# An attention kernel on one core: VectorE planned with its measured pace, and 84 instead of 62 score banks evaluated on it

## The chip, the cores and the metric

The kernel runs on one core of one Trainium2 chip. The metric is the time on the device in microseconds (us), of the whole program. A run is called fast or slow by its state; all runs told here, of every kernel, were in the fast state. Several chips were used, and runs of one call share a chip and the runs of the kernel before on it. PE is TensorE, DVE is VectorE, ACT is ScalarE, POOL is GpSimd, SP is SyncE.

## The reference, cut to what matters

```python
# A: full attention, 16 heads of 28, one shared k and v for all heads; S = 2048, D = 448
q = (x @ wq).reshape(B, S, H, Dh).transpose(0, 2, 1, 3)
k, v = x @ wk, x @ wv
scores = einsum("bhqd,bkd->bhqk", q, k) * Dh ** -0.5
o = einsum("bhqk,bkd->bhqd", softmax(scores), v)
a = o.transpose(0, 2, 1, 3).reshape(B, S, H * Dh) @ wo
# B: sliding attention, 16 heads, window of 8 keys with distance 2, own x, wqkv, wo
b = ...
return concatenate([a, b], axis=-1)
```

A has 16 x 2048 x 2048 exponentials. They decide the time; B is done beside them.

## The kernel before

The scores of A lie in PSUM as 1024 banks of 128 x 512. TensorE writes them into a ring of two slots, of three and of two banks, in turn; one round is both slots. ScalarE reads a slot and writes the exponentials in bf16. 64 banks (one chunk of 512 rows, four heads) are a group; there are 16 groups of about 27 us each.

In some rounds the third bank of the larger slot goes to VectorE, which evaluates the exponential by arithmetic on the bits: one eviction per bank, then three operations of 1024 columns for each two banks. `OFF_AT` says in which rounds of which group:

```python
OFF_AT = {q: (0, 2, 5, 7) for q in range(1, 16)}          # four banks in groups 1 to 15
OFF_AT.update({q: (0, 2, 3, 5, 7, 8) for q in (7,)})       # six in group 7; none in group 0: 62
...
def d_exp(self, bank, slot, sib):
    ...
    o = a("dve", t_dve_ps(512), lambda e: e.tensor_scalar(out=xx[...], in0=g.bank(bank),
        scalar1=-128.0 * A2, scalar2=128.0 * (129 + EOFF), op0=ALU.mult, op1=ALU.add),
        R=[("ring", slot)], W=[("d_x", m % 2, h)], pr=-45)
    if h:                                                   # after the second bank of a pair
        a("dve", t_dve_1x(1024), ... scalar_tensor_tensor(out=u, in0=lo, ...), pr=PSTT)
        a("dve", t_dve_1x(1024), ... scalar_tensor_tensor(out=v, in0=u, ...), pr=PSTT)
        a("dve", t_dve_1x(1024), ... scalar_tensor_tensor(out=out, in0=v, ...), pr=PSTT)
```

The order of the instructions on each engine is made when the kernel is built, by a list scheduler in the kernel. It knows each operation's duration only as a booked constant, takes the ready operation with the lowest `pr`, and lets nothing start on VectorE that would run past the next eviction of the ring by more than `EPS`. At run time the orders are fixed, and semaphores do the rest: an operation whose input is late holds up everything behind it on its engine.

```python
class Sched:
    LATS = {"pe": 0.12, "act": 0.18, "dve": 0.08}           # from an end to the waiting engine
    EPS = 0.03
    OWN = 0.06                                              # from an end to the same engine
...
def t_dve_ps(n): return 0.15 + 1.04e-3 * n
def t_dve_1x(n): return Lock(0.16 + 1.04e-3 * n)
def t_dve_2x(n): return Lock(0.16 + 0.52e-3 * n)
```

Three pieces of the start matter below: the load of the larger part of the query weights, which GpSimd issues and which is booked to land 4 us after its issue; the copies `wq4` of these weights; and the evictions of the keys, in four chunks.

```python
a("gp", 1.5, wload(g.wq, g.A_wq, KC, D), ..., W=[("wq", 1)], dsem="i_wq", land=4, pr=-7.5, ninc=2)
...
for t in range(4):
    a("dve", Lock(0.3), ... tensor_copy(out=g.wq4[:, t], in_=g.wq[...]),
      R=[("wq", min(t, 1)), ...], W=[("wq4", t)], pr=-6 if t == 0 else 1.2 + t)
...
for c in range(4):                                          # key chunks
    pr = -9 if c == 0 else c
    a("dve", t_dve_ps(512), ... tensor_copy(out=kc, in_=g.bank(u.bank)), W=[("kT", c)], pr=pr)   # c > 0
```

The queries of a group are made the same way while the group before it runs: four matmuls, an eviction into `qT`, a square, one more matmul, and a second eviction with an addition.

The softmax here doesn't subtract the row's maximum and nothing guards it: scores larger than these inputs give would overflow.

Of the kernel before, what the change touches and what calls it, by code (L numbers as in the profile page):

```python
# [6 lines left out]
ALU = mybir.AluOpType  # L7
# [7 lines left out]
DH = 28  # L15
# [22 lines left out]
A2 = SCALE * 1.4426950408889634  # L38
OFF_AT = {q: (0, 2, 5, 7) for q in range(1, 16)}
OFF_AT.update({q: (0, 2, 3, 5, 7, 8) for q in (7,)})  # L40
OFF_AT[15] = (0, 2, 3, 5)
LATE = 2
PSTT = -1.5
# [51 lines left out]
class Sched:  # L95
    LAT = 0.13
    LATS = {"pe": 0.12, "act": 0.18, "dve": 0.08}
    MODE = 0.09
# [6 lines left out]
    QKT = 0.315  # L105
    EPS = 0.03
    FILL = None
    OWN = 0.06

# [266 lines left out]
def t_dve_ps(n):  # L376
    return 0.15 + 1.04e-3 * n


def t_dve_1x(n):  # L380
    return Lock(0.16 + 1.04e-3 * n)


def t_dve_2x(n):
    return Lock(0.16 + 0.52e-3 * n)

# [13 lines left out]
class Gen:  # L400
# [185 lines left out]
    def loads(self):  # L586
# [23 lines left out]
        for c in range(NCH):  # L610
            for t in range(4):
                a("sp", 1.3, one(lambda e, c=c, t=t: e.dma_start(
                    out=g.xT_B[:, t, 512 * c:512 * c + 512], in_=g.B_x[0, 512 * c:512 * c + 512, XB0[t]:XB0[t] + 128],
                    transpose=True)), W=[("xT_B", c, t)], dsem=f"i_xb{c}.{t}", land=4.5, pr=-16 + c)
        a("sp", 1.2, lambda e: [
# [19 lines left out]
        for t in range(4):  # L635
            a("dve", Lock(0.3), lambda e, t=t: e.tensor_copy(  # L636
                out=g.wq4[:, t, :, :].rearrange("p k (j e) -> p k j e", j=4)[:, :, :, 0:DH],
                in_=g.wq[:, :, KC * t:KC * t + KC].rearrange("p k (j d) -> p k j d", d=DH)),
              R=[("wq", min(t, 1)), "wqz", ("d_x", 0, 0), ("d_x", 0, 1)], W=[("wq4", t)], pr=-6 if t == 0 else 1.2 + t)
# [5 lines left out]
    def a_head(self):  # L645
# [6 lines left out]
        for c in range(NCH):  # L652
# [11 lines left out]
            if c == 0:  # L664
                a("act", t_act(512), lambda e, u=u, ksq=ksq: e.activation(ksq, g.bank(u.bank), ACT.Square),
                  R=[u, "d_u"], W=[("k_sq", c % 2)], use=u, pr=-100)
            else:
                kc = g.kT[:, 512 * c:512 * c + 512]
                a("dve", t_dve_ps(512), lambda e, u=u, kc=kc: e.tensor_copy(out=kc, in_=g.bank(u.bank)),
                  R=[u], W=[("kT", c)], use=u, pr=pr)  # L670
                a("dve", t_dve_2x(512), lambda e, ksq=ksq, kc=kc: e.tensor_tensor(out=ksq, in0=kc, in1=kc, op=ALU.mult),
                  R=[("kT", c), "d_u"], W=[("k_sq", c % 2)], pr=pr)
            a("pe", t_mm(512), lambda e, u=u, ksq=ksq: e.matmul(g.bank(u.bank), g.hq[:, 2, :], ksq, start=False, stop=True, skip_group_check=True),
# [3 lines left out]
                out=kc, in0=g.bank(u.bank), scalar1=g.cols[:, 0:1], scalar2=None, op0=ALU.add),  # L677
              R=["kadd"], W=[("kT", c)], use=u, pr=pr)
            g.kz_ops[c] = [a("dve", Lock(0.29), lambda e, j=j, c=c, kc=kc: e.tensor_scalar(
                out=g.kz[:, j, 512 * c:512 * c + 512], in0=kc, scalar1=g.cols[:, 8 + j:9 + j], scalar2=None, op0=ALU.mult),  # L680
# [5 lines left out]
    def a_tr(self, c):  # L686

        g, a = self, self.s.add
        for kts in ((0,), (1,), (2,), (3,)) if c == 0 else ((0, 1), (2, 3)):
# [7 lines left out]
            for i, kt in enumerate(kts):  # L697
                dst = g.xT_A[:, kt, 512 * c:512 * c + 512]
                src = lambda u=u, i=i: g.psb[:, 1024 * u.bank + 512 * i:1024 * u.bank + 512 * i + 512]
                if c or kt % 2:  # L700
                    a("dve", 0.42, lambda e, src=src, dst=dst: e.tensor_copy(out=dst, in_=src()),
                      W=[("xT", c, kt)], use=u, pr=-2 if c else -9)
                else:
                    a("act", t_act(512), lambda e, src=src, dst=dst: e.activation(dst, src(), ACT.Copy),
                      W=[("xT", c, kt)], use=u, pr=-110)

    def a_v(self, c):
# [12 lines left out]
        for b in range(4):  # L720
# [11 lines left out]
            in1=gc.unsqueeze(2).to_broadcast([128, 4, DH]), op=ALU.mult),  # L732
          R=[("gcol", c), "v_zero"], W=[("v_aug", 0, c)], use=u, pr=pr)
        a("dve", Lock(0.15), lambda e: e.tensor_scalar(
# [194 lines left out]
    def a_quad_end(self, sc, t, hf=None):  # L929
# [12 lines left out]
        pt = g.PV_T[:, t % 2, :].rearrange("p (b e) -> p b e", e=32)  # L942
        a("dve", 0.25, lambda e: e.reciprocal(out=g.rden[:, t % 2, bs], in_=pt[:, bs, DH]), R=kk("PV"), W=kk("rden"), pr=p0)
        a("dve", t_dve_1x(w), lambda e: e.tensor_tensor(
            out=g.oN[:, bs, :], in0=pt[:, bs, :], in1=g.rden[:, t % 2, bs].unsqueeze(2).to_broadcast([128, b, 32]), op=ALU.mult),
          R=kk("PV") + kk("rden"), W=[("oN", x) for x in keys], pr=p0)
        a("dve", 0.12 + 1.04e-3 * w, lambda e: e.transpose(  # L947
            out=g.oTn[:, t, cs], in_=g.oN[:, :, :].rearrange("p b e -> p (b e)")[:, cs]),
# [28 lines left out]
    B0 = 22.0  # L977
    BSTEP = 23.6

# [90 lines left out]
    def b_soft(self, k2):  # L1070
# [8 lines left out]
          R=[("lg2", par, 0), ("lg2", par, 1)], W=[("e_t", par)], pr=-60)  # L1079
        a("dve", t_dve_1x(256), lambda e: e.tensor_reduce(out=g.ssum[:, :, :], in_=ew, axis=AX.X, op=ALU.add),  # L1080
          R=[("e_t", par)], W=["ssum"], pr=pr)
        a("dve", 0.3, lambda e: e.reciprocal(out=mm(g.rs), in_=mm(g.ssum)), R=["ssum"], W=["rs"], pr=pr)
        for b in range(2):
            a("dve", 0.32, lambda e, b=b: e.tensor_tensor(
                out=g.a_n[:, par, b], in0=g.e_t[:, par, b],
# [76 lines left out]
```

## Time and profile before

| kernel before | |
|---|---|
| median of 3 runs | 460.9 us (460.38 to 461.02) |
| span of the profiled run | 458.8 us |
| first exponential starts, last one ends | 12.03 us, 453.04 us |
| stalls between them | 7.1 us |
| rest of the span (tail) | 5.8 us |

The stalls are worked out from the starts in the trace: the time from one ScalarE instruction to the next, less the time when nothing holds it (904 ns for 1024 columns, 1330 for 1536; 306 and 54 for B's and the key sums' small ones). A stall counts here even where the instructions still overlap in the profile, which the column "idle before" does not show. The views that carry the reading stand in the prediction and are not shown twice. One more is needed later, the busy time of each engine in stretches of the span; the columns are the stretch, its length, busy us (and instructions) of PE, PEld, DVE, ACT and POOL, the granted clock, and the transfers.

```profile
0.00:27.00 27.00, 23.24 (x178) 9.88 (x179) 17.17 (x52) 18.85 (x21) 14.15 (x35) 1.00 1.08 202
27.00:54.00 27.00, 25.12 (x195) 8.61 (x193) 16.31 (x29) 27.00 (x28) 0.40 (x2) 1.00 0.25 43
54.00:441.00 387.00, 367.81 (x3318) 143.06 (x3317) 335.67 (x526) 386.92 (x371) 0.00 (x0) 1.00 0.16 52
```

From 27 us on ScalarE has no gap at all at this scale, and in the first 54 us VectorE is busy for a good half of the time.

### The profile page before, as it was taken

The page shows a single profiled execution, that of the slowest core. Times are in us where ns is not written, and L with a number is a line of the kernel's source. Part 1 is how long each engine was busy: PE and PEld are TensorE (multiplying, and loading weights), DVE is VectorE, ACT ScalarE, POOL GpSimd, SP SyncE. Part 2 cuts the span into 40 slices and gives each one's busy share as a digit, 9 for nine tenths or more (in the row PEclk, how much of TensorE's full clock was granted, in tenths as well). Part 3 has the DMA queues.
Part 4 walks back from the last instruction along what each step waited for, and adds up shares of the span by engine and source line. Part 5 has one row for each costly group of instructions (what it writes and reads, how often), then busy time and mean ns, then how long its engine had stood idle before and what let it go on. Part 6 is the DMA issues. An engine that isn't in the chain of part 4 may idle for free.

```text
span 458.8 us, 8985 instructions
## 1 busy us (share of the span) xinstructions
PE 427.7 (93%) x3818; PEld 165.8 (36%) x3818; DVE 373.9 (81%) x617; ACT 445.3 (97%) x429; POOL 14.6 (3%) x37
## 2 busy tenths in 40 slices
PE   7999898899999999999999999999998998989984
PEld 3333232323542433224243434424233443424331
DVE  5754878989899896988989889998989887896852
ACT  3999999999999999999999999999999999999995
POOL 8300000000000000000000000000000000000000
PEclk9999999999999999999999999999999999999999
DMA  9982112001401230003030302202002032200001
GB/s 178 246 115 36 52 42 100 1 1 47 132 15 61 81 101 11 1 3 99 1 101 31 110 11 85 99 10 82 31 1 90 24 120 91 91 11 10 13 6 36
DMA packets 39987, 27.30 MB, mean 59 GB/s; under 512 B 15518, under 2 KB 39592, under 8 KB 39948
## 3 DMA queue, kind: packets, MB, share of 16 engines
q1 hardware_dynamic: 37452, 24.06, 19.1%
q0 software_dynamic: 816, 1.53, 1.4%
q10 hardware_dynamic: 1680, 1.13, 1.0%
q8 instruction: 30, 0.49, 0.4%
q14 instruction: 9, 0.07, 0.1%
HBM read 18.06 MB, written 5.52 MB: 51 GB/s over the span
## 4 chain that ended last, share of the span: by engine, by line
ACT 93%; PE 4%; DMA 1%; DVE 1%; ACTq 0%; issue 0%
ACT expT L832 92%; DMA stage<-in_A_x_dram 1%; PE ps L1103 1%; PE ps L815 1%; PE ps L812 1%; PE ps L878 1%; ACT e_t L1078 1%; PE ps L961 0%; ACTq L594 0%; PE ps L1052 0%; DVE qT L769 0%; DVE kT L676 0%; ACTq L593 0%; ACT outA L968 0%; ACTq L595 0%
## 5 line engine op out<-in xcount | busy, mean ns | idle before, releaser
L832 ACT ACTIVATE expT<-ps 128x1024 bf16<-128x1024 f32 (+1 forms) x410 | 439.8, 1222 | 2.3 <-PE ps L815 2.2
L815 PE MATMUL ps<-qT,kT 32*128 32x512 bf16 (+1 forms) x859 | 120.8, 373 | 10.9 <-ACT expT L832 8.2
L878 PE MATMUL ps<-expT,v_aug 128*32 128x512 bf16 (+1 forms) x1022 | 95.2, 376 | 0.2 <-ACT expT L832 0.2
L812 PE MATMUL ps<-qT,kz 128*128 128x512 bf16 (+1 forms) x229 | 62.0, 363 | 9.6 <-ACT expT L832 9.1
L815 PEld LDWEIGHTS ps<-qT,kT 32*128 32x128 bf16 x859 | 30.1, 91 | 92.3 <-ACT expT L832 71.4
L911 DVE TENSOR_SCALAR d_x<-ps 128x512 f32<-128x512 f32 x62 | 42.6, 687 | 20.3 <-PE ps L815 19.4
L878 PEld LDWEIGHTS ps<-expT,v_aug 128*32 128x32 bf16 x1022 | 24.5, 93 | 59.8 <-issue 57.1
L1043 DVE TENSOR_TENSOR stage<-qTB,kTB 112x1024 bf16<-112x1024 bf16 x64 | 41.8, 677 | 2.1 <-PE ps L1052 2.1
L1103 PE MATMUL ps<-ident,prod 128*112 128x128 bf16 x512 | 43.5, 224 | 0.1
L1103 PEld LDWEIGHTS ps<-ident,prod 128*112 128x112 bf16 x512 | 34.7, 129 | 16.2 <-issue 12.9
L1002 PE MATMUL ps<-xT_B,wqkv 128*128 128x512 bf16 x128 | 40.4, 383 | 0.0
L1097 DVE TENSOR_TENSOR prod<-Vsh,a_n 128x896 bf16<-128x896 bf16 x64 | 37.3, 613 | 2.5 <-PE ps L1103 2.5
L922 DVE SCALAR_TENSOR_TENSOR d_u<-d_u,d_x 128x1024 f32<-128x1024 f32 x31 | 37.6, 1214 | 0.2
L924 DVE SCALAR_TENSOR_TENSOR dexp<-d_u,d_x 128x1024 int16<-128x1024 f32 x31 | 37.6, 1213 | 0.1
L920 DVE SCALAR_TENSOR_TENSOR d_u<-d_x 128x1024 f32<-128x1024 uint16 x31 | 37.5, 1210 | 0.1
L812 PEld LDWEIGHTS ps<-qT,kz 128*128 128x128 bf16 x229 | 15.0, 97 | 29.5 <-ACT expT L832 27.4
L1052 PEld LDWEIGHTS ps<-ones,stage 112*128 112x128 bf16 x512 | 18.5, 96 | 8.8 <-issue 4.1
L1052 PE MATMUL ps<-ones,stage 112*128 112x4 bf16 x512 | 21.4, 167 | 0.0
L751 PE MATMUL ps<-xT_A,wq 128*128 128x512 bf16 x64 | 20.0, 384 | 0.7 <-DVE wq L636 0.4
L1110 PE MATMUL ps<-wo_B,oT 112*128 112x448 bf16 x64 | 18.5, 357 | 0.3 <-DVE oT L1106 0.2
L938 DVE STREAM_TRANSPOSE PV_T<-ps 128x512 f32<-128x512 f32 (+1 forms) x17 | 11.5, 679 | 8.4 <-PE ps L878 8.3
L961 PE MATMUL ps<-wo,oTn 128*128 128x448 bf16 x64 | 16.8, 356 | 1.4 <-DVE oTn L947 1.4
(105 smaller groups left out, 310.1 us busy)
## 6 DMA issues: line engine op xcount, KB each, us to landing
Vsh<-v_scratch SPq DMA_DIRECT2D x16, 896.0 KB, 4.8
v_scratch<-Vst SPq DMA_DIRECT2D x16, 112.0 KB, 1.7
out_dram<-outB SPq DMA_DIRECT2D x16, 112.0 KB, 1.7
out_dram<-outA SPq DMA_DIRECT2D x15, 112.0 KB, 1.7
stage<-in_A_x_dram ACTq DMA_DIRECT2D x2, 448.0 KB, 5.3
wqkv<-in_B_wqkv_dram SPq DMA_DIRECT2D x1, 672.0 KB, 8.2
wo_B<-in_B_wo_dram POOLq DMA_DIRECT2D x4, 98.0 KB, 5.6
wo<-in_A_wo_dram POOLq DMA_DIRECT2D x4, 98.0 KB, 6.5
```

Source lines behind the costliest of these rows:

```text
L812: r = e.matmul(g.bank(b0 + i, nq, nq * k), g.kz[:, j, 128 * tb:128 * tb + 128], g.qT[:, sc % 2, t, q0:q0 + nq], start=True, stop=True)
L815: r = e.matmul(g.bank(b0 + i, nq, nq * k), g.kT[32 * j:32 * j + 32, 128 * tb:128 * tb + 128], g.qT[32 * j:32 * j + 32, sc % 2, t, q0:q0 + ...
L832: x = a("act", t_exp(w), lambda e, b0=b0, w=w, n=n: e.activation(g.expT[:, n % ERING, 0:w], g.ps[:, 512 * b0:512 * b0 + w], ACT.Exp, scale ...
L878: x = e.matmul(g.bank(PVBANK, nq, q0, p0=32 * j, p1=32 * j + 32), g.v_aug[:, w, tb, :], src[:, nq * k:nq * k + nq], start=first, stop=last ...
L911: o = a("dve", t_dve_ps(512), lambda e: e.tensor_scalar(out=xx[:, 512 * h:512 * h + 512], in0=g.bank(bank), scalar1=-128.0 * A2, scalar2=1 ...
L920: a("dve", t_dve_1x(1024), lambda e: e.scalar_tensor_tensor(out=u, in0=lo, scalar=EP * F, in1=lo, op0=ALU.add, op1=ALU.mult), R=di, W=["d_ ...
L922: a("dve", t_dve_1x(1024), lambda e: e.scalar_tensor_tensor(out=v, in0=u, scalar=EQ * F * F, in1=lo, op0=ALU.add, op1=ALU.mult), R=["d_u"] ...
L924: a("dve", t_dve_1x(1024), lambda e: e.scalar_tensor_tensor(out=out, in0=v, scalar=EL / F ** 3, in1=xx, op0=ALU.mult, op1=ALU.subtract), R ...
L1002: a("pe", t_mm(512), lambda e, u=u, t=t, kt=kt, w=w: e.matmul(g.bank(u.bank), g.wqkv[:, kt, w * D + KC * t:w * D + KC * t + 128], g.xT_B[: ...
L1043: op = a("dve", t_dve_2x(1024), lambda e, t=t, qv=qv, kv=kv: e.tensor_tensor(out=g.prodT[0:KC, t, :, :], in0=qv, in1=kv, op=ALU.mult), R=R ...
L1052: r = e.matmul(g.bank(u.bank, 128).rearrange("p (h w) -> p h w", w=WIN)[:, 4 * t:4 * t + 4, w], g.prodT[0:KC, t, w, :], g.ones4[:, :], sta ...
L1103: a("pe", 0.056, lambda e, u=u, t=t, w=w: e.matmul(g.bank(u.bank, 128, 128 * t, p1=KC), g.prod2[:, w, KC * t:KC * t + KC], g.ident[:, :], ...
```

## The change

It intends two things. The constants with which VectorE is planned become what the trace shows from start to start, so that the plan no longer holds instructions apart that overlap on the chip. The room found so takes 22 more score banks: ten groups with six (group 7, the one that had six, falls back to four), and four in group 0, which had none. Beside these, the evictions of the keys get a higher priority, B's stages a pace of 23.0 in place of 23.6, and B's transposing loads wait for the first half of A's input.

```diff
-OFF_AT = {q: (0, 2, 5, 7) for q in range(1, 16)}
-OFF_AT.update({q: (0, 2, 3, 5, 7, 8) for q in (7,)})
+SIX = (1, 2, 3, 5, 6, 8, 9, 11, 12, 14)
+OFF_AT = {q: (0, 2, 3, 5, 7, 8) if q in SIX else (0, 2, 5, 7) for q in range(1, 16)}
 OFF_AT[15] = (0, 2, 3, 5)
+OFF_AT[0] = (7, 8, 9, 10)
@@
-    LATS = {"pe": 0.12, "act": 0.18, "dve": 0.08}
+    LATS = {"pe": 0.12, "act": 0.18, "dve": 0.165}
-    EPS = 0.03
+    EPS = -0.04
-    OWN = 0.06
+    OWN = 0.02
@@
 def t_dve_ps(n):
-    return 0.15 + 1.04e-3 * n
+    return 0.067 + 1.04e-3 * n
 def t_dve_1x(n):
-    return Lock(0.16 + 1.04e-3 * n)
+    return Lock(0.067 + 1.04e-3 * n)
 def t_dve_2x(n):
-    return Lock(0.16 + 0.52e-3 * n)
+    return Lock(0.067 + 0.52e-3 * n)
@@ B's transposing loads
-                    transpose=True)), W=[("xT_B", c, t)], ..., land=4.5, pr=-16 + c)
+                    transpose=True)), R=[("xst", 0)], W=[("xT_B", c, t)], ..., land=4.5, pr=-16 + c)
@@ key chunks; four operations get such a priority, the last of them an eviction of values
-                  R=[u], W=[("kT", c)], use=u, pr=pr)
+                  R=[u], W=[("kT", c)], use=u, pr=min(pr, -2))
@@
-    BSTEP = 23.6
+    BSTEP = 23.0
 (cut: single durations of VectorE's small operations, 0.03 to 0.12 us lower, but for one that is 0.07 us higher)
```

The two intentions hang together. With the old constants and 84 banks (80 too) the scheduler finds no end and gives up; that is a fact of the build, and no run of it exists.

More of the change, by code (lines that the diff above doesn't have):

```diff
@@ L613, in loads @@
                     out=g.xT_B[:, t, 512 * c:512 * c + 512], in_=g.B_x[0, 512 * c:512 * c + 512, XB0[t]:XB0[t] + 128],
-                    transpose=True)), W=[("xT_B", c, t)], dsem=f"i_xb{c}.{t}", land=4.5, pr=-16 + c)
+                    transpose=True)), R=[("xst", 0)], W=[("xT_B", c, t)], dsem=f"i_xb{c}.{t}", land=4.5, pr=-16 + c)
         a("sp", 1.2, lambda e: [
@@ L635, in loads @@
         for t in range(4):
-            a("dve", Lock(0.3), lambda e, t=t: e.tensor_copy(
+            a("dve", Lock(0.2), lambda e, t=t: e.tensor_copy(
                 out=g.wq4[:, t, :, :].rearrange("p k (j e) -> p k j e", j=4)[:, :, :, 0:DH],
@@ L669, in a_head @@
                 a("dve", t_dve_ps(512), lambda e, u=u, kc=kc: e.tensor_copy(out=kc, in_=g.bank(u.bank)),
-                  R=[u], W=[("kT", c)], use=u, pr=pr)
+                  R=[u], W=[("kT", c)], use=u, pr=min(pr, -2))
                 a("dve", t_dve_2x(512), lambda e, ksq=ksq, kc=kc: e.tensor_tensor(out=ksq, in0=kc, in1=kc, op=ALU.mult),
-                  R=[("kT", c), "d_u"], W=[("k_sq", c % 2)], pr=pr)
+                  R=[("kT", c), "d_u"], W=[("k_sq", c % 2)], pr=-2)
             a("pe", t_mm(512), lambda e, u=u, ksq=ksq: e.matmul(g.bank(u.bank), g.hq[:, 2, :], ksq, start=False, stop=True, skip_group_check=True),
@@ L677, in a_head @@
                 out=kc, in0=g.bank(u.bank), scalar1=g.cols[:, 0:1], scalar2=None, op0=ALU.add),
-              R=["kadd"], W=[("kT", c)], use=u, pr=pr)
-            g.kz_ops[c] = [a("dve", Lock(0.29), lambda e, j=j, c=c, kc=kc: e.tensor_scalar(
+              R=["kadd"], W=[("kT", c)], use=u, pr=min(pr, -2))
+            g.kz_ops[c] = [a("dve", Lock(0.265), lambda e, j=j, c=c, kc=kc: e.tensor_scalar(
                 out=g.kz[:, j, 512 * c:512 * c + 512], in0=kc, scalar1=g.cols[:, 8 + j:9 + j], scalar2=None, op0=ALU.mult),
@@ L700, in a_tr @@
                 if c or kt % 2:
-                    a("dve", 0.42, lambda e, src=src, dst=dst: e.tensor_copy(out=dst, in_=src()),
+                    a("dve", 0.335, lambda e, src=src, dst=dst: e.tensor_copy(out=dst, in_=src()),
                       W=[("xT", c, kt)], use=u, pr=-2 if c else -9)
@@ L732, in a_v @@
             in1=gc.unsqueeze(2).to_broadcast([128, 4, DH]), op=ALU.mult),
-          R=[("gcol", c), "v_zero"], W=[("v_aug", 0, c)], use=u, pr=pr)
+          R=[("gcol", c), "v_zero"], W=[("v_aug", 0, c)], use=u, pr=-2)
         a("dve", Lock(0.15), lambda e: e.tensor_scalar(
@@ L942, in a_quad_end @@
         pt = g.PV_T[:, t % 2, :].rearrange("p (b e) -> p b e", e=32)
-        a("dve", 0.25, lambda e: e.reciprocal(out=g.rden[:, t % 2, bs], in_=pt[:, bs, DH]), R=kk("PV"), W=kk("rden"), pr=p0)
+        a("dve", 0.16, lambda e: e.reciprocal(out=g.rden[:, t % 2, bs], in_=pt[:, bs, DH]), R=kk("PV"), W=kk("rden"), pr=p0)
         a("dve", t_dve_1x(w), lambda e: e.tensor_tensor(
@@ L946, in a_quad_end @@
           R=kk("PV") + kk("rden"), W=[("oN", x) for x in keys], pr=p0)
-        a("dve", 0.12 + 1.04e-3 * w, lambda e: e.transpose(
+        a("dve", 0.09 + 1.04e-3 * w, lambda e: e.transpose(
             out=g.oTn[:, t, cs], in_=g.oN[:, :, :].rearrange("p b e -> p (b e)")[:, cs]),
@@ L1079, in b_soft @@
           R=[("lg2", par, 0), ("lg2", par, 1)], W=[("e_t", par)], pr=-60)
-        a("dve", t_dve_1x(256), lambda e: e.tensor_reduce(out=g.ssum[:, :, :], in_=ew, axis=AX.X, op=ALU.add),
+        a("dve", Lock(0.5), lambda e: e.tensor_reduce(out=g.ssum[:, :, :], in_=ew, axis=AX.X, op=ALU.add),
           R=[("e_t", par)], W=["ssum"], pr=pr)
-        a("dve", 0.3, lambda e: e.reciprocal(out=mm(g.rs), in_=mm(g.ssum)), R=["ssum"], W=["rs"], pr=pr)
+        a("dve", 0.26, lambda e: e.reciprocal(out=mm(g.rs), in_=mm(g.ssum)), R=["ssum"], W=["rs"], pr=pr)
         for b in range(2):
-            a("dve", 0.32, lambda e, b=b: e.tensor_tensor(
+            a("dve", 0.2, lambda e, b=b: e.tensor_tensor(
                 out=g.a_n[:, par, b], in0=g.e_t[:, par, b],
```

## The prediction

> **What bounds the kernel now.** I read the chain that ended last first, then the busy shares, then the Activate groups with shapes kept apart, then who waited for whom, then VectorE's timeline.
>
> ```profile
> PE 427.7 (93%) x3818; PEld 165.8 (36%) x3818; DVE 373.9 (81%) x617; ACT 445.3 (97%) x429; POOL 14.6 (3%) x37
> ...
> ACT 93%; PE 4%; DMA 1%; DVE 1%; ACTq 0%; issue 0%
> ```
>
> Two views say the same: ScalarE is busy 97% of the span, and 93% of the chain of waits is ScalarE, nearly all of it the exponential of the score banks (line 832). TensorE's 93% counts pipelined matmuls and fillers, so I don't take it for the bound. The Activate groups by shape, in the columns count, busy time, mean of one, idle before:
>
> ```profile
> L832 ACT ACTIVATE expT<-ps 128x1024 bf16<-128x1024 f32 x266 | 267.7, 1077 | 0.1
> L832 ACT ACTIVATE expT<-ps 128x1536 bf16<-128x1536 f32 x143 | 214.0, 1497 | 2.2 <-PE ps L815 2.2
> ```
>
> Each round takes three banks and then two. Where VectorE takes the third bank of a round, the 1536-wide Activate becomes a 1024-wide one; none disappears. The idle time before them is 2.3 us in all, and that is the start. Activates overlap, so small delays hide in that view: from the starts in the trace, one takes 904 ns (1024 wide) or 1330 ns (1536 wide) to the next start when nothing holds it, and the sum of what lies above that is **7.1 us of small stalls**, spread evenly over the loop. The first exponential starts at 12.03 us and the last ends at 453.04; what follows is the tail.
>
> VectorE's own waits, and a stretch of its timeline (start, duration, instruction):
>
> ```profile
> DVE d_x L911 <- PE ps L815: 19.4, 31, 2.4
> ```
> ```profile
> 129.61 0.69 DVE L911 TENSOR_SCALAR d_x<-ps 128x512 f32<-128x512 f32 x1
> 130.22 0.68 DVE L1043 TENSOR_TENSOR stage<-qTB,kTB 112x1024 bf16<-112x1024 bf16 x1
> 130.81 1.22 DVE L920 SCALAR_TENSOR_TENSOR d_u<-d_x 128x1024 f32<-128x1024 uint16 x1
> 131.95 0.61 DVE L1113 CAST outB<-ps 128x448 bf16<-128x448 f32 x1
> 132.49 1.21 DVE L922 SCALAR_TENSOR_TENSOR d_u<-d_u,d_x 128x1024 f32<-128x1024 f32 x1
> ```
>
> The eviction at 129.61 lasts 0.69 us, yet the next instruction starts 0.61 us later; the 1.22 us one is followed after 1.14. Each lasts about 80 ns into the next. The kernel orders its engines with its own list scheduler, and that booked 0.68 us for such an eviction and 1.22 for the wide one. So VectorE runs ahead of its plan and then stands: half of its 62 evictions of score banks (31) wait for TensorE, 19.4 us together.
>
> **What the Trainium skill says.** "Vector Engine (DVE) Microarchitecture Reference", section 5.2 Measured stream behaviour on trn2: built-in VectorE operations cost 1.0417 ns per column plus about 75 ns each after queue overlap; that gives 608 ns for 512 columns and 1142 for 1024. The trace agrees: medians of start to start are 608 and 1132. "Perfetto Trace Analysis", section Per-instruction lifecycle: the reported end of a VectorE or ScalarE instruction is the write's acknowledgement, while the next may begin earlier; so durations add up to more than the engine's real occupation. That is what the timeline shows. "ScalarE: Activation LUTs", section What ACT_TABLE_LOAD costs: an Activate takes 0.833 ns per element; the 512 elements that go make 427 ns, and the trace's two periods differ by 426. "DMA: Bandwidth & Descriptors", section Issuing engines are not separate DMA queues: transfers from any engine interleave on the same 16 DMA engines. The first slice of the page has them at 9 tenths.
>
> **The change part by part.**
> 1. *Score banks from ScalarE to VectorE, 62 to 84.* Built, the changed kernel has 121 Activates of 1536 and 288 of 1024 (143 and 266 before). 22 shrink: 22 x (1497 - 1077) = **9.2 us** (9.4 by start to start). All of this is on the path, as long as ScalarE stays bound.
> 2. *Its price on VectorE.* 22 more evictions (22 x 0.608 = 13.4 us) and 11 more triples of wide operations (33 x 1.132 = 37.4 us): **50.7 us**, off the path as long as it fits. It is tight. From 30 to 450 us VectorE is busy 352.4 us of 420 (sums of windows). Some 47 us of the addition fall there, in a stretch 9 us shorter: about 399 of 411, or 97% by durations. Taking 80 ns off each overlapped instruction, I counted 359 us of true occupation in the whole span before; 410 after is 91% of some 450, and around 94% in the loop. Part of the room comes from the first group of heads, where VectorE was working only 15 us in each of the first two stretches of 27 us; four of the new banks lie there.
> 3. *New estimates for the scheduler.* Constants close to the measured start to start (0.60 and 1.13 us), a later landing (0.165 us) so that the completion stays where it was, and 70 ns more margin before each deadline of the score ring (from +0.03 to -0.04 us). It costs nothing and removes waits that come from a wrong plan. It is also the condition for part 2: with the old estimates 50 us more would not have fitted.
> 4. *TensorE.* Fillers (matmuls on zeros) fall from 77 to 65 and the full-array score matmuls from 229 to 170, replaced by row-tiled ones. Nothing needed is added. Small relief.
> 5. *Start.* Three transposing loads of B's input used to be issued at 1.95 us, in between the loads A starts with. They now wait for the first half of A's input. The second half landed 6.69 us after its issue (2.74 to 9.43), and it stands in the chain in front of the first exponential. An extra copy of 0.34 us is put between the two evictions that release the first scores, against three transposes moved out of the way. I book **0.7 us** gained, between -0.3 and 1.5.
> 6. *Tail.* The last group keeps its four banks. In the new order B's last output copy comes just before the last half's transpose, instead of well before it; no row of B is left after A's end. I book 0.
>
> Sum: 460.9 - 9.2 - 0.7 = 451.0 with the 7.1 us of stalls unchanged. I choose +0.5 for a fuller VectorE net of the better plan: **451.5 us**, 2.0% less.
>
> **Rivals.**
> - *VectorE becomes the bound.* Then evictions of the third bank come late, the next scores for these banks wait, and ScalarE waits for TensorE. For it: 94% occupation in a fixed order, six groups in which VectorE has more to do than the group lasts, so B's work must slide. Against it: the plan knows the true durations and puts ring evictions first; in the built order B's work still ends in time. If half of the thirteen stretches lost 0.5 to 1 us each, it would be 455 to 457.
> - *The better plan also removes old stalls.* The 7.1 us include many of 60 to 200 ns where scores came just late; 70 ns more margin could take 2 to 3 us of them: 448.5 to 449.5.
> - *TensorE takes over.* It is 93% busy and the same matmuls must fit into 9 us less. Against it: 12 fillers and 59 full-array matmuls go, and 71.4 us of waits of weight loads for ScalarE are left to give. I give this 1 us at most.
> - *The start's gain does not come*, since A's own transposing loads now start earlier and press on the second half: 452.
>
> **Range and chances.** The lower end has both old stalls removed and the start gained: 460.9 - 9.4 - 1.0 - 2.3 = 448.2. The upper end has VectorE late in most groups: 456. 2% lies at 451.7, almost on my figure, so faster and same are nearly even; I lean to faster since the constants look fitted on traces. A loss of over 2% would need 18 us of new stalls.
>
> **What would show it.** Right: 121 Activates of 1536 columns; ScalarE still about 93% of the chain; VectorE near 424 us busy by the page (94%), its waits for score banks well under 19 us; stalls between exponentials near 7 us; the first exponential at 11 to 12 us. Wrong: stalls of 12 us and more with VectorE's eviction of scores late and weight loads waiting for it; a chain in which VectorE or TensorE has 10% or more; a first exponential later than 12.5 us; more than 6 us between the last exponential and the end.

## The result, and the profile after

The changed kernel took **455.4 us** (median of four runs: 455.56, 455.24, 456.64, 453.01), the kernel before 460.96 us (four runs, 460.38 to 462.23). The ratio is 0.987, with a 95% interval of 0.982 to 0.992: within 2%. Ratios are the mean time of one kernel's fast runs over that of the other's of the same rounds, so not quite the ratio of the medians. The time lies within the predicted range, 4 us above the figure. The profiled run has a span of 453.5 us and a granted clock of 0.99, and the one run at 453.01 had 0.996.

From the page of the changed kernel, the busy line, the granted clock of TensorE in 40 slices, and the shares of the chain that ended last:

```profile
PE 421.9 (93%) x3806; PEld 165.2 (36%) x3806; DVE 417.2 (92%) x672; ACT 435.5 (96%) x429; POOL 14.4 (3%) x37
...
PEclk9899999999999999999999999999999999999997
...
ACT 90%; DVE 4%; PE 2%; POOL 1%; DMA 1%; issue 0%; POOLq 0%
```

VectorE has gone from 81% to 92%, ScalarE from 445.3 to 435.5 us, and the chain now has 4% of VectorE where it had 1%. The second slice of the clock is an 8, the only one before the end. The exponentials by shape, and VectorE's wait for score banks:

```profile
L833 ACT ACTIVATE expT<-ps 128x1024 bf16<-128x1024 f32 x288 | 292.1, 1136 | 2.1 <-PE ps L813 1.5 <-PE ps L879 0.7
L833 ACT ACTIVATE expT<-ps 128x1536 bf16<-128x1536 f32 x121 | 188.6, 1559 | 3.7 <-PE ps L816 3.6
```
```profile
DVE d_x L912 <- PE ps L816: 1.9, 4, 1.2
```

The counts are as built. The means of one went up by 59 and 62 ns; the period from start to start did not, 904 and 1330 ns remain the medians. So a longer mean here is not a slower instruction, and I read the pace from the starts. What is new is the idle time: 5.8 us before exponentials, for 2.3. VectorE's evictions hardly wait any more (4 of 84, where it was 31 of 62). In the middle of the kernel its timeline has no gaps:

```profile
129.40 0.68 DVE L1044 TENSOR_TENSOR stage<-qTB,kTB 112x1024 bf16<-112x1024 bf16 x1
130.00 0.70 DVE L948 STREAM_TRANSPOSE oTn<-oN 128x512 bf16<-128x512 bf16 x1
130.68 0.69 DVE L912 TENSOR_SCALAR d_x<-ps 128x512 f32<-128x512 f32 x1
131.30 0.69 DVE L1107 CAST oT<-ps 112x512 bf16<-112x512 f32 x1
131.91 1.22 DVE L921 SCALAR_TENSOR_TENSOR d_u<-d_x 128x1024 f32<-128x1024 uint16 x1
```

The same stretches of the span as before show where the time is lost:

```profile
0.00:27.00 27.00, 23.04 (x157) 9.98 (x158) 16.48 (x48) 16.99 (x20) 13.69 (x34) 0.94 0.97 160
27.00:54.00 27.00, 24.75 (x199) 8.45 (x197) 23.89 (x41) 24.70 (x29) 0.69 (x3) 1.00 0.56 84
54.00:441.00 387.00, 366.50 (x3378) 144.50 (x3376) 373.41 (x577) 387.00 (x378) 0.00 (x0) 1.00 0.16 52
```

Beyond 54 us ScalarE is as full as before, although VectorE is at 373.4 of 387 us. In the first 27 us ScalarE is busy 1.9 us less and the clock is at 0.94; in the next 27 us it is busy 2.3 us less at full clock. The count from the starts agrees (us):

| | first exponential | stalls to 27 | 27 to 54 | beyond | tail | span |
|---|---|---|---|---|---|---|
| before | 12.03 | 0.27 | 0.57 | 6.26 | 5.8 | 458.8 |
| after | 11.74 | 2.58 | 3.00 | 5.46 | 6.2 | 453.5 |
| difference | -0.29 | +2.31 | +2.43 | -0.80 | +0.4 | -5.3 |

What is missing in the sum is ScalarE's work without stalls: 433.9 us before (453.04 - 12.03 - 7.10) and 424.6 after (447.33 - 11.74 - 11.04), so **9.3 us saved** (22 x 0.426 = 9.4). It came in full. 4.7 us of it were given back in two places of the first 54 us. They are two separate episodes.

**Episode A, 15 to 21 us.** VectorE's timeline of the changed kernel (the bracket is the idle time before and what ended it):

```profile
12.16 1.51 DVE L680 TENSOR_SCALAR kz<-kT,cols 128x512 bf16<-128x512 bf16 x4
14.44 0.28 DVE L637 COPY wq<-d_x 128x448 bf16<-128x448 bf16 x1 [0.78 <-DMA d_x<-in_A_wq_dram]
14.63 0.68 DVE L670 CAST kT<-ps 128x512 bf16<-128x512 f32 x1
```

The order puts a copy of query weights, which nothing needs for another 15 us, in front of the eviction of the second key chunk. The weights landed at 14.42 us; the plan had them at 11.8, and in the kernel before they landed at 12.28. There the copies also stood in front of the same eviction, and waited for nothing:

```profile
13.03 0.49 DVE L636 COPY wq<-d_x 128x448 bf16<-128x448 bf16 x2
14.50 0.69 DVE L669 CAST kT<-ps 128x512 bf16<-128x512 f32 x1 [0.28 <-PE ps L659]
```

So in the changed kernel VectorE stands, the keys are late, TensorE stands for 1.11 us up to 15.89, and then its clock falls. The windows of one us, in the columns told above:

```profile
16.00:17.00 1.00, 1.00 (x12) 0.40 (x10) 0.70 (x2) 0.43 (x2) 0.00 (x0) 1.00 0.90 123
17.00:18.00 1.00, 1.00 (x5) 0.41 (x5) 0.89 (x4) 1.00 (x1) 0.00 (x0) 0.67 1.07 151
18.00:19.00 1.00, 1.00 (x4) 0.23 (x3) 0.59 (x3) 0.60 (x3) 0.00 (x0) 0.50 1.67 153
19.00:20.00 1.00, 1.00 (x4) 0.30 (x2) 0.27 (x1) 0.88 (x1) 0.20 (x1) 0.50 0.96 93
20.00:21.00 1.00, 1.00 (x8) 0.18 (x7) 0.39 (x1) 0.00 (x0) 0.00 (x0) 0.63 1.26 121
```

For 3.4 us (17.33 to 20.74) TensorE ran at half clock, with scores as its only urgent work, and ScalarE stalled at 15.3, 16.9 and 18.9 us (0.71, 0.52 and 1.28 us). The Trainium skill, "TensorE: Matmul & The Clock Gate", Part 1: The HAM clock gate, describes a gate that halves the clock after an idle window of about 3.4 us and gives it back after as long a busy one. The length agrees (3.4 us). The condition does not: TensorE had stood for 1.11 us in one piece, and was busy 2.10 of the 3.4 us before the fall.

**Episode B, 34 to 43 us.** VectorE again, then TensorE and ScalarE:

```profile
37.98 0.68 DVE L762 CAST qT<-ps 128x512 bf16<-128x512 f32 x1
38.58 1.21 DVE L921 SCALAR_TENSOR_TENSOR d_u<-d_x 128x1024 f32<-128x1024 uint16 x1
39.72 0.42 DVE L764 TENSOR_TENSOR q_sq<-qT 128x512 bf16<-128x512 bf16 x1
40.05 1.22 DVE L923 SCALAR_TENSOR_TENSOR d_u<-d_u,d_x 128x1024 f32<-128x1024 f32 x1
41.19 0.74 DVE L770 TENSOR_SCALAR qT<-ps,cols 128x512 bf16<-128x512 f32 x1
```
```profile
41.98 0.60 PE L813 MATMUL ps<-qT,kz 128*128 128x512 bf16 x2 [1.05 <-DVE qT L770]
```
```profile
42.63 6.46 ACT L833 ACTIVATE expT<-ps 128x1024 bf16<-128x1024 f32 x6 [1.48 <-PE ps L813]
```

The queries of the second group are on a chain (`qT`, `q_sq`, `qT`), and between its links VectorE does the wide operations of the four banks that group 0 now has. The queries are ready at 41.9 us, TensorE has waited 1.05 us for them, and ScalarE 1.48. With two smaller stalls at 34.0 and 39.8 us this is nearly all of the 3.0 us. In the kernel before, the second group's queries were ready some 6.6 us earlier, and only then VectorE stood:

```profile
34.56 0.75 DVE L769 TENSOR_SCALAR qT<-ps,cols 128x512 bf16<-128x512 f32 x1 [0.48 <-PE ps L765]
39.66 0.27 DVE L730 TENSOR_TENSOR v_aug<-ps,gcol 128x112 bf16<-128x112 f32 x1 [4.34 <-ACT gcol L726]
```

The room was there, but behind the queries. The scheduler saw most of this coming: its own plan has ScalarE standing for 2.1 us between 27 and 54 us, with one gap of 1.42; in the plan before it was 0.15.

### The profile page after: what moved, and what is told of

It is laid out like the page before. It is cut to its first block, busy times and chain, and to the rows that moved or that the text cites. A ratio compares the mean times of both kernels' runs of the same rounds, so it can differ in the third digit from the quotient of the medians.

```text
span 453.5 us, 9035 instructions
## 1 busy us (share of the span) xinstructions
PE 421.9 (93%) x3806; PEld 165.2 (36%) x3806; DVE 417.2 (92%) x672; ACT 435.5 (96%) x429; POOL 14.4 (3%) x37
## 4 chain that ended last, share of the span: by engine, by line
ACT 90%; DVE 4%; PE 2%; POOL 1%; DMA 1%; issue 0%; POOLq 0%
ACT expT L833 90%; DMA d_x<-in_A_wq_dram 1%; PE ps L660 1%; DVE d_x L912 1%; ACT e_t L1079 1%; DVE d_u L921 1%; DVE d_u L923 0%; PE ps L813 0%; PE ps L816 0%; PE ps L436 0%; DVE kz L680 0%; DVE kT L670 0%; DVE dexp L925 0%; PE ps L962 0%; POOL wv L594 0%
## 5 line engine op out<-in xcount | busy, mean ns | idle before, releaser
L833 ACT ACTIVATE expT<-ps 128x1024 bf16<-128x1024 f32 (+1 forms) x410 | 429.9, 1260 | 5.8 <-PE ps L816 3.6
L816 PE MATMUL ps<-qT,kT 32*128 32x512 bf16 (+1 forms) x918 | 130.5, 372 | 13.7 <-ACT expT L833 10.6
L879 PE MATMUL ps<-expT,v_aug 128*32 128x512 bf16 (+1 forms) x1000 | 90.1, 376 | 1.4 <-ACT expT L833 1.0
L912 DVE TENSOR_SCALAR d_x<-ps 128x512 f32<-128x512 f32 x84 | 57.3, 682 | 2.1 <-PE ps L816 1.9
L813 PE MATMUL ps<-qT,kz 128*128 128x512 bf16 (+1 forms) x170 | 47.6, 370 | 7.1 <-ACT expT L833 5.4
L921 DVE SCALAR_TENSOR_TENSOR d_u<-d_x 128x1024 f32<-128x1024 uint16 x42 | 51.0, 1214 | 0.2
L923 DVE SCALAR_TENSOR_TENSOR d_u<-d_u,d_x 128x1024 f32<-128x1024 f32 x42 | 51.0, 1215 | 0.1
L925 DVE SCALAR_TENSOR_TENSOR dexp<-d_u,d_x 128x1024 int16<-128x1024 f32 x42 | 51.0, 1215 | 0.1
L1104 PEld LDWEIGHTS ps<-ident,prod 128*112 128x112 bf16 x512 | 34.0, 129 | 14.7 <-issue 11.7
L813 PEld LDWEIGHTS ps<-qT,kz 128*128 128x128 bf16 x170 | 10.9, 97 | 23.9 <-ACT expT L833 21.1
L1018 PE MATMUL ps<-wqv,xT_B 128*128 128x448 bf16 x64 | 18.1, 356 | 0.9 <-DVE kTB L1008 0.5
```

Of the source, the lines that this page charges most:

```text
L813: r = e.matmul(g.bank(b0 + i, nq, nq * k), g.kz[:, j, 128 * tb:128 * tb + 128], g.qT[:, sc % 2, t, q0:q0 + nq], start=True, stop=True)
L816: r = e.matmul(g.bank(b0 + i, nq, nq * k), g.kT[32 * j:32 * j + 32, 128 * tb:128 * tb + 128], g.qT[32 * j:32 * j + 32, sc % 2, t, q0:q0 + ...
L833: x = a("act", t_exp(w), lambda e, b0=b0, w=w, n=n: e.activation(g.expT[:, n % ERING, 0:w], g.ps[:, 512 * b0:512 * b0 + w], ACT.Exp, scale ...
L879: x = e.matmul(g.bank(PVBANK, nq, q0, p0=32 * j, p1=32 * j + 32), g.v_aug[:, w, tb, :], src[:, nq * k:nq * k + nq], start=first, stop=last ...
L921: a("dve", t_dve_1x(1024), lambda e: e.scalar_tensor_tensor(out=u, in0=lo, scalar=EP * F, in1=lo, op0=ALU.add, op1=ALU.mult), R=di, W=["d_ ...
L923: a("dve", t_dve_1x(1024), lambda e: e.scalar_tensor_tensor(out=v, in0=u, scalar=EQ * F * F, in1=lo, op0=ALU.add, op1=ALU.mult), R=["d_u"] ...
```

## The experiments

The theory has two halves: the missing 4 us are episode A (late weights, in front of the keys, and the clock that falls then) and episode B (the four banks in front of the next group's queries), and the rest of the change does what was booked. The rival: VectorE is full, and the stalls are the price of its 84 banks wherever they lie. Where the recorded expectations give numbers and say nothing else, theory 1 is about episode A and theory 2 about episode B. Twelve runs were made in three calls, each call on one chip; two of the twelve are the changed kernel again. Edits are against the changed kernel. All results were correct.

### First call: episode A

**The changed kernel again** (no edit), as the base of this chip.

> The changed kernel unaltered, on the same chip as the three that follow, so that they are compared with it. Expected 455.5 us, 453 to 457; sum of stalls between exponentials 9.5 to 11.5 us, of which 5 to 6 in the first 54 us; TensorE's clock granted at half speed somewhere between 16 and 21 us.

Measured 452.9 us, ratio 0.984 (0.982 to 0.987). Its five runs fall into two sorts, by the granted clock: 456.18 and 455.72 us at 0.993, and 452.93, 452.83, 452.64 us at 0.996 to 0.999. So this kernel has two times, some 3 us apart, within the fast state. The profiled run was of the first sort: the weights landed at 15.55 us, VectorE waited 2.6 us for them, and the stalls of the first 27 us were 4.39 us. Episode B was the same as in the first comparison (3.01 us). So episode A is a matter of the chip and of the run; that the three faster runs lacked it is inferred from their clock, since they have no trace. The median missed the expected 453 to 457 us by a little, and the stalls of the profiled run, 12.8 us in all, lay above the expected 9.5 to 11.5.

**The copies of the weights behind the keys** (the load is booked later, which moves three copies on VectorE and, by one place, one matmul of the second key chunk on TensorE).

```diff
-..., W=[("wq", 1)], dsem="i_wq", land=4, pr=-7.5, ninc=2)
+..., W=[("wq", 1)], dsem="i_wq", land=7.5, pr=-7.5, ninc=2)
```


> Only the three copies of the query weights for heads 4 to 15 move on VectorE: behind the eviction of the second key chunk instead of in front of it (the scheduler is told that this load lands 3.5 us later). TensorE's order and everything else stay. Theory 1 (VectorE stands in its order for a load of weights that nobody needs before 32 us, TensorE starves behind it for about 1 us, its clock is then halved for about 3 us, and ScalarE loses 2.4 us): the stalls of the first 27 us fall from 2.6 us to under 1 us, the clock stays at 1.0, and the time falls by 2 to 2.5 us to about 453. Rival (the key load of A's third chunk, or simply more DMA traffic, holds the start): the copies' place is of no account, under 0.7 us gained, and the stall near 19 us stays.

Measured 453.2 us, ratio 0.984 (0.981 to 0.986). In its trace episode A is gone: no wait for the weights, stalls up to 27 us 0.72, full clock there. But 4.32 us lie between 27 and 54: TensorE's pause of 1.05 us for the queries, at 38.4 to 39.5, was followed by the half clock here (0.54, 0.50, 0.50, 0.75 in the four windows from 40 us), which it was not in the changed kernel. Part of the gain reappears as a worse episode B, and the medians do not resolve the rest. So this run shows what makes episode A, but not the gain in time that was expected.

**Five matmuls on zeros ahead of the pause**, so that TensorE is busier before it.

```diff
+                def vm(e, u=u, b=b, tb=tb, kt=kt):
+                    for _ in range(5 if (c, b, kt) == (0, 2, 2) else 0):
+                        e.matmul(g.bank(PVBANK), g.warm[:, 0:128], g.warm[:, :], start=True, stop=True)
+                    return e.matmul(...)                    # the matmul that was here
```


> The changed kernel with five extra matmuls on zeros put into TensorE's order just before the 1.1 us in which it stands at 14.8 to 15.9 us; no wait is taken away and no other order changes. If it is the clock that makes the larger part of the loss (half clock from 17.3 to 20.6 us), the clock stays near 1.0, the stall of 1.3 us near 19 us goes while those near 15 and 17 us (1.2 us together) stay, and the time falls by 1.0 to 1.6 us. If the loss is the late load itself and the clock only accompanies it, nothing is gained: 0 to 0.3 us, or slightly slower.

Measured 454.4 us, ratio 0.986 (0.984 to 0.988). The clock was 1.00 from 15 to 21 us and the early stalls were 1.15 us, although VectorE still waited 0.7 us for the weights. Against the changed kernel's first profile, with 2.58 us of stalls and a wait of 0.78 us, the half clock makes about 1.4 us, the larger part. That is not so where the weights are later: of the 4.39 us in this chip's profile of the changed kernel, 2.73 us lie in one stall, most of it before the clock falls at 17.80 us. The later stalls were 4.32 us, as above, with a half clock at the same pause, and the 1.0 to 1.6 us expected were not won.

**B's loads not held back**.

```diff
-                    transpose=True)), R=[("xst", 0)], W=[("xT_B", c, t)], ...
+                    transpose=True)), W=[("xT_B", c, t)], ...
```


> The changed kernel with the new condition on the loads of B's input taken away again: three of them are issued at 1.95 us as in the kernel before; no compute engine's order changes. My prediction booked 0.7 us gained by the condition. If the condition, which lets A's own transposing loads start about 1 us earlier and pile up on the weights, is what made the query weights land late (14.4 us instead of 12.3), then without it they land near 12.3 us, the first exponential comes 0.3 us later, and the time falls by 1.5 to 2.5 us net. If the landing time has nothing to do with it, the time rises by 0.3 to 1 us.

Measured 453.8 us, ratio 0.986 (0.984 to 0.989), against 452.9 for the changed kernel on this chip: 0.9 us slower by the medians, with intervals that overlap. The weights landed at 12.80 us and the early stalls were 0.26, but the second half of A's input landed at 9.74 us instead of 7.22, and the first exponential started at 14.9 us, behind a stretch of half clock from 8.85 to 12.26 us. So the expectation came half true: without the gate the weights landed earlier than in the three traces with it on this chip (13.65 to 15.55 us), but no time was won by it. That the gate is worth the 0.7 us that the prediction booked is not shown.

### Second call: episode B and the number of banks

On this chip the weights landed at about 12.0 us in every trace (11.73 to 12.05), so episode A does not occur in them. The kernel before took 460.84 us (27 runs).

**Two banks in group 0 instead of four, earlier; group 7 gets six again.** The sum stays at 84.

```diff
-SIX = (1, 2, 3, 5, 6, 8, 9, 11, 12, 14)
+SIX = (1, 2, 3, 5, 6, 8, 9, 11, 12, 14, 7)
-OFF_AT[0] = (7, 8, 9, 10)
+OFF_AT[0] = (6, 8)
```


> The changed kernel with the same 84 banks placed otherwise: the first group gives up two rounds (rounds 6 and 8 in place of 7, 8, 9, 10), the eighth group takes two more. The load of the query weights stays as it is. Theory 2 (VectorE's work on the first group's four banks delays the queries of heads 4 to 7, so that ScalarE stands for about 3 us around 34 to 42 us, by the scheduler's own booking for the most part): the stalls between 27 and 54 us fall from 3.0 us to under 1.2 us, and the time falls by 1.7 to 2.5 us against the control's 452.9, to about 451. Rival (the four banks were only in the way because the start had run late): stalls there stay above 2 us and the time within 0.8 us of the control.

Measured **451.44 us** (451.3 to 451.88), ratio 0.979 (0.977 to 0.981). The stalls between 27 and 54 us are 0.98 instead of 3.0, and ScalarE is busy 26.6 of these 27 us:

```profile
27.00:54.00 27.00, 25.90 (x194) 8.34 (x194) 22.15 (x36) 26.63 (x28) 0.40 (x2) 1.00 0.34 62
```

With as many banks on VectorE as the change has, the time falls by 9.4 us (460.84 - 451.44). ScalarE's work without stalls gives 9.2 of it (433.9 less 424.7); the first exponential 1.2 us earlier and a tail 1.0 us longer nearly cancel, and the stalls are 0.25 us less. The rival falls for 84 banks.

**The same with the copies behind the keys.**

```diff
-OFF_AT[0] = (7, 8, 9, 10)                                    # and group 7 in SIX
+OFF_AT[0] = (6, 8)
-..., W=[("wq", 1)], dsem="i_wq", land=4, pr=-7.5, ninc=2)
+..., W=[("wq", 1)], dsem="i_wq", land=7.5, pr=-7.5, ninc=2)
```

> Both: the query weights' copies behind the second key chunk, and the first group's banks at rounds 6 and 8 with two more in the eighth. Each alone left or caused a pause of TensorE of about 1 us, and a halved clock after it. Expected, if both pauses and the clock are the whole loss: stalls under 2 us in the first 54 us, the clock at 1.0 throughout the loop, and 448.5 to 450.5 us, over 2% faster than the kernel before. If a pause only moves on to the next weak place, as it did when one of them was taken away: 451.5 to 453.

Measured 451.44 us (451.35 to 451.62), ratio 0.979. The stalls were 1.3 us in the first 54 us and the clock was 1.00, as the first expectation asks, but its 448.5 to 450.5 us were missed. Where the weights land early, the place of the copies costs and brings nothing.

**No banks in group 0** (80 in all).

```diff
-OFF_AT[0] = (7, 8, 9, 10)
```


> The changed kernel without banks on VectorE in the first group: 80 in all. ScalarE gets 4 x 0.426 = 1.7 us more to do. Theory 2: the stalls between 27 and 54 us fall from 3.0 us to under 1 us, which outweighs the 1.7 us: 452 to 453 us, the same as the control or a little better. If the four banks are worth their 1.7 us and cost nothing: 454.5 us.

Measured 455.9 us (455.48 to 456.21), ratio 0.989 (0.987 to 0.991). The stalls between 27 and 54 us are 0.64, as the theory of episode B has it, but the time missed the 452 to 453 us that I had expected. ScalarE has 4 x 0.426 = 1.7 us more to do (its last exponential ends at 445.3 us, and at 442.4 in the kernel with two banks in group 0), the stalls beyond 54 us are 6.4 us instead of 5.3, and the tail is 8.6 us instead of 6.8: rows of B are left over, and VectorE still has them among the last evictions of A. So another order of B may well have cost 2 us at the end, which the count of stalls does not hold; that it was B is read from the trace and was not tested alone.

**The new plan with the old 62 banks.**

```diff
-SIX = (1, 2, 3, 5, 6, 8, 9, 11, 12, 14)
+SIX = (7,)
-OFF_AT[0] = (7, 8, 9, 10)
```


> The kernel before's 62 banks, with the changed kernel's estimates, priorities and loads: everything but the move of banks. My prediction booked for this 0.7 us at the start and no loss: 460.2 us. If the new order alone carries the loss at the start (late weights, halved clock), it shows here too: stalls of 2 to 3 us in the first 27 us, and 461 to 463 us. If the new estimates by themselves take away stalls in the loop (from 5.8 us beyond 54 us to 4.5 or less): 458 to 459.5.

Measured 461.03 us (22 runs, 460.83 to 467.65), ratio 1.002 (1.000 to 1.004). The runs fall into two sorts here too: 16 at 460.83 to 461.47 us, and six at 463.6 to 467.7 with a granted clock of 0.986 to 0.992. The slower sort has no trace; its clock looks like the changed kernel's slower sort, so the new plan may bring it without the banks, and an early landing in one trace does not exclude it in other runs. The plan alone brings nothing. In the profiled run, of the faster sort, the first exponential starts at 10.83 us, 1.2 us earlier than in the kernel before, but the stalls are 8.28 us instead of 7.10. The whole gain is the banks', and the plan is what lets them be built.

### Third call: the landing, and the limit

The kernel before took 461.07 us (11 runs).

**The changed kernel again**, on this chip.

> The changed kernel again, as the measure for the other three on their chip. On one chip the small piece of the query weights landed at 14.4 to 15.6 us, on another one kernels with the same start had it at 12.0. Late here: 453 to 456 us in two groups, with a halved clock in the slower one. Early here: no stall over 0.5 us in the first 27 us, 452.5 to 453.5 us, since the 3 us of stalls between 27 and 54 us remain.

Measured 452.86 us (452.16 to 453.72), ratio 0.983 (0.981 to 0.984). The weights landed at 12.34 us, the early stalls were 0.51, episode B's 2.88; so episode B does not need a late start. Without episode A, it takes about what its faster sort took on the first chip.

**The weights made late on purpose, with the copies in front of the keys.** This is the kernel with two banks in group 0; the load is issued behind those of B, and its booking is such that all orders of computing instructions stay as they were.

```diff
-OFF_AT[0] = (7, 8, 9, 10)                                    # and group 7 in SIX, as above
+OFF_AT[0] = (6, 8)
-..., W=[("wq", 1)], dsem="i_wq", land=4, pr=-7.5, ninc=2)
+..., W=[("wq", 1)], dsem="i_wq", land=-1.5, pr=2.05, ninc=2)
-            for j in range(4)], W=["wo4"], dsem="i_wo4", land=5, pr=2, rel=4, ninc=4)
+            for j in range(4)], W=["wo4"], dsem="i_wo4", land=5, pr=2.1, rel=4, ninc=4)
```


> The placing at rounds 6 and 8 (451.4 us), with the load of the query weights issued behind two other weight loads, so that it lands late on any chip (estimate 17 us or later); the order of every compute engine is exactly that of the 451.4 us kernel, with the copies in front of the second key chunk. Theory 1: VectorE waits for the load, TensorE stands, its clock is halved: stalls of 3 to 6 us in the first 27 us and 454.5 to 458 us. If the place of the copies is of no account: within 0.7 us of 451.4.

Measured 460.72 us (459.59 to 462.0), ratio 0.999 (0.997 to 1.001). The load landed at 20.70 us, and VectorE's timeline and the windows of the span show episode A enlarged:

```profile
20.73 0.28 DVE L637 COPY wq<-d_x 128x448 bf16<-128x448 bf16 x1 [7.58 <-DMA d_x<-in_A_wq_dram]
20.92 0.68 DVE L670 CAST kT<-ps 128x512 bf16<-128x512 f32 x1
```
```profile
16.00:20.00 4.00, 0.00 (x0) 0.00 (x0) 0.00 (x0) 0.00 (x0) 0.00 (x0) 0.50 1.15 158
20.00:24.00 4.00, 1.82 (x12) 0.62 (x12) 2.69 (x7) 0.19 (x1) 0.00 (x0) 0.50 1.08 162
24.00:28.00 4.00, 4.00 (x14) 1.07 (x13) 1.58 (x5) 2.35 (x3) 0.20 (x1) 0.50 1.54 230
```

The early stalls are 10.33 us, more than the 3 to 6 us expected, and so is the time.

**The weights as late, with the copies behind the keys**: the edit above, but for one number.

```diff
-..., W=[("wq", 1)], dsem="i_wq", land=4, pr=-7.5, ninc=2)
+..., W=[("wq", 1)], dsem="i_wq", land=10, pr=2.05, ninc=2)
```

> The same late load, but the three copies stand behind the third key chunk on VectorE, where even a load that lands at 20 us keeps nobody waiting. Theory 1: the late load costs nothing then: under 1 us of stalls in the first 27 us, the clock at 1.0, 451 to 452 us, 3 us or more under the run with the copies in front. If late landing itself or the crowded start is the cost, it is as slow as that run.

Measured 451.5 us (451.26 to 451.82), ratio 0.980 (0.978 to 0.981). The load landed at 20.43 us, and held up nothing:

```profile
12.99 0.68 DVE L670 CAST kT<-ps 128x512 bf16<-128x512 f32 x1
...
22.77 0.46 DVE L637 COPY wq<-d_x 128x448 bf16<-128x448 bf16 x2
```

The early stalls are 0.57 us. Between these two kernels lie 9.2 us, by nothing but the place of three copies in VectorE's order (and again one matmul by one place). That shows the mechanism of episode A. On the same chip this kernel is 1.4 us faster than the changed kernel (451.5 against 452.86), which is episode B's part in time; the 1.9 us that the stalls between 27 and 54 us fell by are partly taken by a tail of 6.8 instead of 5.8 us.

**88 banks**: six in groups 1 to 14, four in group 15, none in group 0, with the copies behind the keys (`land=7.5`).

```diff
-SIX = (1, 2, 3, 5, 6, 8, 9, 11, 12, 14)
+SIX = (1, 2, 3, 4, 5, 6, 7, 8, 9, 10, 11, 12, 13, 14)
-OFF_AT[0] = (7, 8, 9, 10)
```


> 88 banks on VectorE: six in each group but the first and last, none in the first. It tests my first rival, VectorE as the bound. ScalarE's work falls by 4 x 0.426 = 1.7 us against 84 banks; 2 more triples of wide operations make 9.2 us more VectorE work. If VectorE has room left: about 450 us. If it is at its limit, ScalarE still ends about 1.5 us earlier, near 441 us, but B's last rows are left over and VectorE works them off after the last exponential: a tail of 12 us or more in place of 6.8, and 456 us or more.

Measured 464.2 us (463.25 to 465.56), ratio 1.007 (1.005 to 1.009). ScalarE's last exponential ends at 440.6 us, 1.8 us earlier than in the best kernel; the stalls are 7.1 us. But the span ends 20.6 us later:

```profile
441.00:462.00 21.00, 14.68 (x159) 9.52 (x156) 13.51 (x28) 0.96 (x2) 0.00 (x0) 1.00 0.27 88
```

ScalarE has 0.96 us to do in this stretch and VectorE 13.5, 21 of its 28 instructions for rows of B that it had not done before. At 88 banks VectorE sets the end, though not in the way of the rival: the ring's evictions keep their place, and B pays. Between 84 and 88 nothing was run.

## Why the prediction was right or wrong

- **ScalarE's saving (9.2 to 9.4 us, on the path): right.** 9.3 us in the profile, and 9.2 us in the kernel with two banks in group 0, whose time fell by 9.4.
- **The price on VectorE, off the path as long as it fits: right beyond 54 us, wrong before.** True occupation, by durations less what overlaps the next instruction (80 ns), is 408.6 us for the booked 410; 373.4 of 387 us between 54 and 441 is 96.5% for the booked 97%; ScalarE's stalls there fell by 0.8 us. The step that failed is the sentence "Part of the room comes from the first group of heads, where VectorE was working only 15 us in each of the first two stretches of 27 us". It counted the room as a sum over 27 us. The trace of the kernel before had much of that room behind the second group's queries (4.34 us in one piece); the four banks came in front of them. It cost 2.4 us of stalls (episode B). The forecast had the plan at hand, which itself showed 2.1 us of it.
- **The start (0.7 us gained, -0.3 to 1.5): the gain came, and more was lost beside it.** The first exponential started 0.29 us earlier in the profiled run and 0.7 to 1.2 us earlier in all later ones with the gate; that this was the gate's doing is not shown (0.9 us by the medians on the chip of the first call, not resolved). What the step left out is that the copies of the weights lay in front of the keys: 2.3 us of stalls in the profiled run, about 3 us between the two sorts of runs. I had looked at the loads that stand in the chain of the kernel before; this one was not in it, since it landed early enough there.
- **The stalls (+0.5 us net): the term that was mis-sized.** It measured +3.9 us: +2.3, +2.4 and -0.8. 451.0 with +3.9 and the tail's +0.4 is 455.3, next to the median of 455.4; with the start's measured 0.3 for 0.7 and 9.3 for 9.2 it is 455.6, the time of the profiled run. That 455.4 lies in the range is in part luck: the upper end of 456 stood for VectorE late in most groups, and what cost the 4 us was in two places of the first 54 us that the sum did not have.
- **The tail (0):** 0.4 us more.
- **The rivals.** VectorE as the bound did not happen at 84 banks (two of group 0's banks earlier and two in group 7 instead give the whole gain) and did at 88. Old stalls removed by the plan: 0.8 us beyond 54 us instead of 2 to 3, and none with 62 banks. TensorE taking over: seen only as the half clock after its pauses. "The start's gain does not come" named another load than the one that was late.
- **The signs.** 121 wide Activates, the first exponential at 11 to 12 us and the small wait for score banks (1.9 us) were there. VectorE was busy 417 us instead of 424, ScalarE had 90% of the chain instead of 93%, and the stalls were 11.0 us instead of 7, near the mark set for wrong, but with the eviction of scores on time. The tail, 6.2 us, was just over the 6 us set for wrong. The chain had 4% of VectorE, under the mark of 10%.
- **The chances** leaned to faster; the changed kernel ended within 2%. A corrected order of the same change, 451.4 to 451.5 us, is 2.1% faster than the kernel before, with intervals that reach over the mark of 2%.

The 608, 1142 and 427 ns that the prediction works out from the Trainium skill's figures are estimates; the trace had 608, 1132 and 426, and the sums use these.

Open remain three things. The first is why the weights land late on some chips: at 11.7 to 12.3 us in all traces with this issue on two of them, at 13.65 to 15.55 on the third with the gate and at 12.80 there without it, in one trace. In the first comparison too, the kernel before, without the gate, had 12.28 and the changed kernel 14.42. So the gate may have a part in it, together with the chip.

The second is why a pause of TensorE is followed by the half clock in one kernel and not in another. The same 1.05 us before the second group's queries stands in all six traces with four banks in group 0, and the half clock comes with it in two, late_wq and warm. The traces show that the clock keeps a grid: each short stretch of half clock lasted 3.41 us, the one of 13.65 us four times that, and all of them begin a whole number of such steps before the last fall of their trace (126 steps in the changed kernel, 119 in late_wq). The changed kernel's pause lies across a line of its grid (41.23 us), and late_wq's inside one step, with TensorE busy 2.36 us of it. But the pause in the run called control lay inside one step too, with 2.36 us busy, and the clock stayed. So the place in the grid may matter and does not decide it alone.

The third is why the best orders have a tail 1 us longer.

## What to carry to other kernels

An engine's free time counts only where it lies: before new work is put into it, look at what stands behind that place in the engine's order, and whether that ends in the bound engine's next input. In a fixed order, nothing that waits for a transfer should stand in front of urgent work unless it is needed as soon; here the place of some copies of 0.2 us was worth 9.2 us when the load was late. Where a scheduler in the kernel makes the order, read the gaps in its own plan before running it, and book with start-to-start times; here the plan with 84 banks could be built only with the new constants.

## What the Trainium skill lacked or had wrong

- "TensorE: Matmul & The Clock Gate", Part 1: it asks for an idle window of about 3.4 us before the clock is halved. Here the clock was halved for 3.4 us after a pause of 1.11 us, with TensorE busy 2.10 of the 3.4 us before it, and in another kernel after one of 1.05 us with 2.35 busy; an equal pause in the changed kernel did not do it. The page also tells of clocks that fall with many short idle times, but gives no measure that tells these cases apart.
- "ScalarE: Activation LUTs", What ACT_TABLE_LOAD costs: it gives an overlap of about 93 ns for Activates back to back. The trace of the kernel before shows durations of 1077 and 1497 ns at periods of 904 and 1330 ns, so about 170 ns for these, which read PSUM.
- No page that I read says how far the landing of one small load varies: the same piece of weights (42 KB) landed from 11.7 to 15.6 us in kernels that issue it at 8.4 to 8.6 us.
